# A decode step with K and V of 2048 rows streamed through a ring: the first rows of wq, V0's rows of P, the groups of the last w4 rows and the banks of the final sums

## Chip, cores and metric

One core of a Trainium2 chip. The metric is the device time of one execution in microseconds. The kernel before takes 212.08 us (median of three runs, 212.0 to 212.32); one more execution, taken with the hardware profiler, took 211.53 us.

## The reference

Four rows x (4 x 576) are normalised to xn. The result is x + A(xn) + B(xn):

```python
q = (x @ wq).reshape(B, Sq, Hq, Dh).transpose(0, 2, 1, 3)
k = jnp.repeat(k_cache[:, :, Sk - W:, :], rep, axis=1)
v = jnp.repeat(v_cache[:, :, Sk - W:, :], rep, axis=1)
p = softmax(einsum("bhqd,bhkd->bhqk", q, k) * Dh ** -0.5)
A = einsum("bhqk,bhkd->bhqd", p, v).transpose(0, 2, 1, 3).reshape(B, Sq, Hq * Dh) @ wo
B = x1 + gelu(layernorm(x1) @ w3) @ w4
```

Here W is 2048, Dh 128, with 32 query heads on 16 cache heads and 4 sequences; F is 4608. With one row per sequence the four shifted parts of the mixer (g0 to g3) are zero, so hs is zero, x1 is xn, and w1 and w2 are not needed. wq is 576 x 4096, wo 4096 x 576, w3 576 x 4608, w4 4608 x 576, all bf16. K and V give 33.5 MB each, the four matrices 20 MB: 87 MB are read for a few KB of result.

## The kernel before

All large inputs go through one SBUF tile, `ring`, by transfers that SP issues one after the other (L113, L500, L577). In order: wq in two pieces, w3, eight K tiles, two pairs of V tiles, four single V tiles, wo, 18 rows of w4, and w4's other 18 rows in groups of 7, 6, 3 and 2 (a row here is one of the 36 rows of w4 that a partition holds; the last two come in two column halves). A cache tile is 128 partitions x 32 KB and lies in one of four slots; SP's wait before a transfer is for the last reader of the place it overwrites.

*q.* x is normalised on DVE, cast, copied apart and transposed by PE (L188 to L203) into `xnT`. 36 matmuls of 512 columns (L233) add q up in one PSUM bank, in half rows of wq: wq lies in SBUF with 4.5 rows in a partition, so each half row has its own columns of `xnT`.

*K.* DVE transposes each K tile in four operations (L292), PE adds the scores up in four banks S0 to S3 (L301), one for each K tile of a half of the heads.

*P and V.* ACT takes four exponentials (L344, one per bank). `pick_rows` (L350) is eight matmuls of 512 columns that bring P's rows to the partitions on which V's rows lie; `keep_rows` (L358) copies them to `CB` on ACT; `spread_rows` (L367) makes a block matrix X from them in four DVE operations, and `v_compute` (L380) runs 64 matmuls of 256 columns for a V tile. X has two buffers. From L534 on, the order on PE, ACT and DVE is the order of the program text.

*The order behind V2.* PE zeroes a second bank ACC2 (L554); x + xn lies in the first bank, ACC, since the start (L271). The GELU of w3's product, and for the second half of the heads `heads_out`, `heads_rows` and `heads_pick`, lead to 64 matmuls with wo (L433), and from there to w4.

*The end.* `acc_matmuls` (L430) adds a row of wo or w4 to one of the two banks, even rows to ACC and odd ones to ACC2, each row in two halves of 288 columns. Four strips of the array's 128 output rows are in use so, one for each bank and half. For the last rows the sums move to four more banks `SUMS` in quarters of 144 columns: `copy_sums` (L445) copies the two banks to SBUF on ACT and DVE, `quads` (L440) adds the last 3 + 2 rows in quarters, and `merge_sums` (L449) adds the copied sums by f32 matmuls. Four casts and two output transfers (L595 to L600), one on SP and one on ACT, end the kernel.

Of the kernel before, what the change touches and what calls it, by code (L numbers as in the profile page):

```python
# [18 lines left out]
def kernel(  # L19
# [100 lines left out]
    V_order = K_order  # L120

    def k_load(n):
        bp, kq = K_order[n]
        t = ring[:, SLOT[n % 4]:SLOT[n % 4] + TILE]
        lo = Sk - W + kq * 4 * CK
        src = k_rows[MT * bp:MT * bp + MT, lo:lo + 4 * CK, :].rearrange("m (q c) d -> m q (c d)", q=4)
        return load_run(t, src).rearrange("p (c d) -> p c d", d=Dh)
# [3 lines left out]
    def v_load(n, tiles):  # L131

        bp, kq = V_order[n]
        t = ring[:, SLOT[n % 4]:SLOT[n % 4] + tiles * TILE]
        lo = Sk - W + kq // 2 * 8 * CK
        src = v_rows[MT * bp:MT * bp + MT, lo:lo + 8 * CK, :].rearrange("m (q h c) d -> m q h (c d)", q=4, h=2)
        h = kq % 2
        load_run(t, src[:, :, h:h + tiles, :].rearrange("m q h x -> m q (h x)"))
        for i in range(tiles):
            V_tiles[n + i] = t[:, i * TILE:(i + 1) * TILE].rearrange("p (c d) -> p c d", d=Dh)  # L140
# [47 lines left out]
    def transposed_prep(src_bf, name):  # L188

        dup = z_part(2 * NO * P, BF16)[0:B].rearrange("p (e o m) -> p e o m", e=2, o=NO)  # L190
        nc.gpsimd.memset(dup, 0.0)
        for e in range(2):
            nc.vector.tensor_copy(out=dup[:, e, :, e:P:2],  # L193
                                  in_=ap_of(src_bf, e * (NS // 2), [[1, NO], [NS, P // 2]]))
        return dup, const.tile([P, 2 * NO, B], BF16, name=name)

    def transposed_pe(prep):
        dup, T = prep
        tp = ps_tp.tile([P, 2 * NO, B], BF16, tag="tp")
        for o in range(NO):  # L200
            for e in range(2):
                nc.tensor.transpose(out=tp[:, 2 * (NO - 1 - o) + e, :], in_=dup[:, e, o, :], identity=ident[0:B, 0:B])  # L202
        nc.vector.tensor_copy(out=T[:], in_=tp[:])  # L203

    def slot_cols(T, s):

        return T[:, NS - 1 - s:NS + 1 - s, :].rearrange("p e b -> p (e b)")

# [20 lines left out]
    transposed_pe(xn_prep)  # L229
    for s in range(NS):  # L230
        for i in range(QI):
            f0 = s * (NQ // 2) + i * QN
            nc.tensor.matmul(out=qp[32 * i:32 * i + 2 * B, :], lhsT=slot_cols(xn_prep[1], s), rhs=wq_t[:, f0:f0 + QN],  # L233
                             start=False, stop=False, skip_group_check=True)
# [115 lines left out]
    def pick_rows(bp, g0, g1):  # L350
        for r in range(rep):
            if (bp, r) not in CPS:
                CPS[bp, r] = ps_s.tile([P, NG * CK], F32, tag="S", name=f"C{bp}{r}")
            for q in range(4):
                nc.tensor.matmul(out=CPS[bp, r][:, g0 * CK:g1 * CK], lhsT=pick[:, bp, r, 3 - q:3 - q + P],  # L355
                                 rhs=ap_of(Z, g0 * 4 * CK + q * 2 * CK, [[8 * CK, (g1 - g0) // 2], [1, 2 * CK]]), start=(q == 0), stop=(q == 3), skip_group_check=True)
# [21 lines left out]
    V_tiles, O_tiles = {}, {}  # L378

    def v_compute(n):  # L380
        bp, g = V_order[n]
        if g == 0:
# [47 lines left out]
    def acc_matmuls(lhsT, row, half):  # L430
        for q in range(2):
            o0 = 64 * half + 32 * q
            nc.tensor.matmul(out=ACCS[half][o0:o0 + B, 0:DH], lhsT=lhsT, rhs=row[:, q * DH:(q + 1) * DH],  # L433
                             start=False, stop=False, skip_group_check=True)

    SUMS = []

    DQ = D // 4

    def quads(lhsT, rows, qs=range(4), start=False):  # L440
        for q in qs:
            nc.tensor.matmul(out=SUMS[q][32 * q:32 * q + B, 0:DQ], lhsT=lhsT, rhs=rows[:, q * DQ:(q + 1) * DQ],  # L442
                             start=start, stop=False, skip_group_check=True)

    def copy_sums():  # L445
        nc.scalar.copy(out=sums[0:64], in_=ACC[0:64, 0:DH])
        nc.vector.tensor_copy(out=sums[64:P], in_=ACCS[1][64:P, 0:DH])  # L447

    def merge_sums():  # L449
        for q in range(2):  # L450
            for z in range(2):
                g = 2 * q + z
                nc.tensor.matmul(out=SUMS[g][32 * g:32 * g + B, 0:DQ], lhsT=perm[:, q, :],  # L453
                                 rhs=sums[:, z * DQ:(z + 1) * DQ], start=False, stop=False, skip_group_check=True)
# [49 lines left out]
    perm = const.tile([P, 2, B], F32)  # L504
    nc.vector.memset(perm[:].rearrange("p q m -> p (q m)"), 0.0)
    for h in range(2):
        for q in range(2):
            p0 = 64 * h + 32 * q
            nc.vector.tensor_copy(out=perm[p0:p0 + 32, q, :], in_=ident[p0:p0 + 32, p0:p0 + B])

    def mlp_out(t, e, i0, n):
# [22 lines left out]
    with tc.manual_schedule(engines=ENGINES):  # L534
        for g in range(NG):
            exponentials(g)
        pick_rows(0, 0, NG)
# [8 lines left out]
        for n in range(1, NV):  # L546
            v_compute(n)
            if n == 1:
                pick_rows(1, 0, NG)
                keep_rows(1, 0, NG)  # L550
                reciprocal_rows()
            if n == 2:
                ACCS.append(ps_s.tile([P, 512], F32, tag="S", name="ACC2"))
                nc.tensor.matmul(out=ACCS[1][:], lhsT=ident[:], rhs=zeros[:], start=True, stop=False, skip_group_check=True)  # L554
# [10 lines left out]
            if n + 4 < NV:  # L565
                v_load(n + 4, 1)
            if n == 5:
# [6 lines left out]
                last = ring[:, REST + (i0 - E1[0]) * D:REST + (NFH - E1[0]) * D].rearrange("p (i n) -> p i n", n=D)
                for side in range(2):
                    cols = slice(side * DH, (side + 1) * DH)
                    nc.sync.dma_start(out=last[:, :, cols], in_=w4_src[1, :, i0:NFH, cols])  # L577
# [13 lines left out]
        l2, l1 = [(gT[:, 2 * NFH - 2 + i, :], last[:, i, :]) for i in range(2)]
        for (g, t), q in ((l2, 0), (l1, 0), (l2, 1), (l1, 1), (l2, 2), (l2, 3), (l1, 2), (l1, 3)):
            quads(g, t, (q,))

    fins = [const.tile([B, DH], out.dtype, name=f"fin{side}") for side in range(2)]  # L595
    for q, copy in enumerate((nc.scalar.copy, nc.vector.tensor_copy, nc.vector.tensor_copy, nc.scalar.copy)):
        side, z = divmod(q, 2)
        copy(out=fins[side][:, z * DQ:(z + 1) * DQ], in_=SUMS[q][32 * q:32 * q + B, 0:DQ])  # L598
# [32 lines left out]
```

## Time and profile before

| | |
|---|---|
| median of three runs | 212.08 us |
| the profiled execution | 211.53 us |
| its span | 209.6 us |
| PE busy | 123.2 us, 59% |
| DVE busy | 130.1 us, 62% |
| ACT busy | 15.1 us |
| mean granted clock of TensorE | 0.757 |
| bytes read | 87.17 MB, 416 GB/s over the span |
| share of the 16 DMA engines that SP's queue took | 97.0% |
| first transfer issued | 0.74 us |
| K tiles landed | 37.81 to 105.9 us |
| V0 starts, V2 starts, V7 ends | 125.95, 144.56, 190.36 us |
| matmuls with wo, with w4 | from 194.06, from 200.18 us |

How to read it: an execution is measured once, from the first to the last instruction. Busy time is summed for each engine over the span. Behind an instruction in the timeline stand its tiles (out<-in), its shape, and in brackets how long its engine was idle ahead of it and what ended that. DMA shares are means of sixteen engines; in half microseconds they jump, because a packet counts where it ends.

### The profile page before, as it was taken

Reading aid. Unit: us, or ns where it says so; the run is one execution under the profiler, and the core shown is the slowest. Engines: PE = TensorE matmul, PEld = TensorE weight load, DVE = VectorE, ACT = ScalarE, POOL = GpSimd, SP = SyncE. Lnnn points to the kernel's source line nnn. Section 1 sums busy time; section 2 is a strip of 40 time slices with the busy share of each in tenths; the row PEclk is TensorE's granted clock in tenths of the full one; section 3 lists DMA queues with packets and bytes.
Section 4 is the critical chain, followed back from the end, with each engine's and each line's share of the span. In section 5 each row is a group of like instructions: output and inputs, shape, how many; then the busy total and the mean of one; then the engine's idle time right before and its main releaser. Section 6 shows DMA issues by size and latency. Waiting matters only on the chain.

```text
span 209.6 us, 2462 instructions
## 1 busy us (share of the span) xinstructions
PE 123.2 (59%) x1086; PEld 74.2 (35%) x1086; DVE 130.1 (62%) x125; ACT 15.1 (7%) x42; POOL 4.0 (2%) x10
## 2 busy tenths in 40 slices
PE   1234289143535333333333369995999997994762
PEld 0011111011111111111111118874888986883431
DVE  6952100799898989899999229976075599402002
ACT  4002100100000000000000340002001010001001
POOL 6100000000000000000000000000000000000000
PEclk9999999755555555555555559998899999999557
DMA  7998999999999999999999999999999999999991
GB/s 257 438 460 388 460 410 438 444 419 438 444 419 438 436 419 432 450 419 425 469 413 466 488 425 400 400 428 413 444 422 432 444 422 425 437 418 426 421 386 53
DMA packets 3745, 87.31 MB, mean 417 GB/s; under 512 B 396, under 2 KB 920, under 8 KB 1432
## 3 DMA queue, kind: packets, MB, share of 16 engines
q1 hardware_dynamic: 3720, 87.17, 97.0%
q8 instruction: 8, 0.13, 0.2%
q10 hardware_dynamic: 16, 0.01, 0.0%
q14 instruction: 1, 0.01, 0.0%
HBM read 87.17 MB, written 0.00 MB: 416 GB/s over the span
## 4 chain that ended last, share of the span: by engine, by line
DMA 70%; PE 19%; DVE 8%; issue 1%; SPq 1%; DVEq 0%
DMA ring<-in_A_k_cache_dram 29%; DMA ring<-in_B_w_dram 26%; PE O L386 14%; DMA ring<-in_A_v_cache_dram 14%; DVE kt L292 8%; PE G L468 4%; SPq L113 0%; SPq L500 0%; DVE mx L278 0%; PE SUM L442 0%; PE OX L416 0%; DVEq L626 0%; DVE fin L598 0%; PE SUM L453 0%; PE ACC L554 0%
## 5 line engine op out<-in xcount | busy, mean ns | idle before, releaser
L292 DVE STREAM_TRANSPOSE kt<-ring 128x2048 int32<-128x2048 int32 x32 | 71.4, 2283 | 18.7 <-DMA ring<-in_A_k_cache_dram 18.6
L386 PE MATMUL O<-ring,X 128*128 128x256 bf16 x512 | 58.4, 277 | 2.7 <-DVE X L373 1.7
L301 PE MATMUL S<-kt,Z 128*32 128x512 bf16 x256 | 30.4, 622 | 49.7 <-DVE kt L292 49.7
L386 PEld LDWEIGHTS <-X 128*128 128x128 bf16 x512 | 50.6, 99 | 10.4 <-DVE X L373 3.7
L373 DVE TENSOR_TENSOR X<-Z,own 128x1024 int32<-128x1024 int32 x32 | 36.9, 1219 | 18.9 <-issue 8.7
L301 PEld LDWEIGHTS <-Z 128*32 128x32 bf16 x256 | 10.1, 127 | 70.3 <-issue 70.3
L468 PE MATMUL G<-ring,ln2T 128*8 128x512 bf16 (+1 forms) x54 | 10.5, 862 | 2.2 <-DMA ring<-in_B_w_dram 2.2
L421 DVE TENSOR_TENSOR Z<-OX,own_d 128x256 f32<-128x256 f32 x2 | 0.8, 425 | 14.2 <-PE OX L416 14.2
L344 ACT ACTIVATE Z<-S,nb 128x512 bf16<-128x512 f32 x4 | 2.7, 694 | 80.7 <-DVE nb L531 80.7
L447 DVE COPY Z<-ACC 64x288 f32<-64x288 f32 x1 | 0.5, 461 | 12.3 <-PE ACC L433 12.3
L355 PE MATMUL C<-Z,pick 128*128 128x512 bf16 x16 | 5.5, 504 | 3.4 <-ACT Z L344 3.4
L468 PEld LDWEIGHTS <-ln2T 128*8 128x8 bf16 x54 | 2.1, 98 | 11.9 <-issue 11.0
L433 PE MATMUL ACC<-ring,gT 128*4 128x288 bf16 x62 | 3.9, 405 | 3.3 <-DMA ring<-in_B_w_dram 3.2
L202 PE MATMUL tp<-ident,Z 4*128 4x4 bf16 x20 | 1.1, 164 | 7.6 <-DVE Z L193 7.6
L433 PE MATMUL ACC<-ring,onx 128*4 128x288 bf16 x64 | 4.0, 442 | 2.2 <-DMA ring<-in_A_wo_dram 2.2
L233 PE MATMUL qp<-ring,xnT 128*8 128x512 bf16 x36 | 4.2, 621 | 1.7 <-DMA ring<-in_A_wq_dram 1.4
L244 DVE CAST q_rows<-qp 128x256 bf16<-128x256 f32 x4 | 1.5, 420 | 5.5 <-PE qp L233 4.7
L360 ACT CAST Z<-C 128x128 bf16<-128x128 f32 (+2 forms) x6 | 3.0, 543 | 18.0 <-PE C L355 17.9
L355 PEld LDWEIGHTS <-pick 128*128 128x128 bf16 x16 | 1.9, 119 | 6.6 <-issue 5.8
L202 PEld LDWEIGHTS <-Z 4*128 4x128 bf16 x20 | 0.8, 101 | 9.1 <-DVE Z L193 5.6
L433 PEld LDWEIGHTS <-gT 128*4 128x4 bf16 x62 | 2.0, 109 | 5.4 <-issue 4.2
L278 DVE TENSOR_REDUCE mx<-S 128x1 f32<-128x512 f32 x4 | 2.7, 671 | 2.0 <-PE S L301 2.0
(82 smaller groups left out, 47.2 us busy)
## 6 DMA issues: line engine op xcount, KB each, us to landing
ring<-in_A_k_cache_dram SPq DMA_DIRECT2D x8, 4096.0 KB, 35.6
ring<-in_A_v_cache_dram SPq DMA_DIRECT2D x4, 4096.0 KB, 22.3
ring<-in_B_w_dram SPq DMA_DIRECT2D x1, 5184.0 KB, 25.1
ring<-in_A_wo_dram SPq DMA_DIRECT2D x1, 4608.0 KB
ring<-in_A_wq_dram SPq DMA_DIRECT2D x1, 4096.0 KB
ring<-in_B_w_dram SPq DMA_DIRECT2D x1, 2592.0 KB, 26.8
ring<-in_B_w_dram SPq DMA_DIRECT2D x1, 1008.0 KB, 27.5
ring<-in_B_w_dram SPq DMA_DIRECT2D x1, 864.0 KB, 29.3
```

What stands on the lines that cost most here:

```text
L202: nc.tensor.transpose(out=tp[:, 2 * (NO - 1 - o) + e, :], in_=dup[:, e, o, :], identity=ident[0:B, 0:B])
L233: nc.tensor.matmul(out=qp[32 * i:32 * i + 2 * B, :], lhsT=slot_cols(xn_prep[1], s), rhs=wq_t[:, f0:f0 + QN], start=False, stop=False, skip ...
L278: nc.vector.reduce_max(out=mx[:, g:g + 1], in_=S[g][:], axis=AX.X)
L292: nc.vector.transpose(out=ap32(kt[e], c0 * 2 * G, [[2 * G, C2 // 2], [1, 2], [2, G]]), in_=ap32(kn, c0 * 4 * G + e * G, [[4 * G, C2 // 2], ...
L301: nc.tensor.matmul(out=S[kq][c:c + 32, :].rearrange("p (c q l) -> p c q l", q=4, l=2), lhsT=qz[:, bp, m, y, :], rhs=kt[e][:, :, 4 * m:4 * ...
L344: nc.scalar.activation(out=EP[:, g].rearrange("p q (c l) -> p c q l", l=2), in_=S[g][:].rearrange("p (c q l) -> p c q l", q=4, l=2), func= ...
L355: nc.tensor.matmul(out=CPS[bp, r][:, g0 * CK:g1 * CK], lhsT=pick[:, bp, r, 3 - q:3 - q + P], rhs=ap_of(Z, g0 * 4 * CK + q * 2 * CK, [[8 * ...
L360: nc.scalar.copy(out=CB[:, bp, g0:g1, :, r], in_=CPS[bp, r][:, g0 * CK:g1 * CK].rearrange("p (g c) -> p g c", c=CK))
L373: nc.vector.tensor_tensor(out=ap32(X, a * CX * MT, [[MT, CX], [1, MT]]), in0=bass.AP(s32.tensor, s32.offset, [list(s32.ap[0]), [1, CX], [0 ...
L386: nc.tensor.matmul(out=O_tiles[bp][:], lhsT=X[:, c:c + 2, :].rearrange("p c n -> p (c n)"), rhs=vn[:, c:c + 2, :].rearrange("p c d -> p (c ...
L433: nc.tensor.matmul(out=ACCS[half][o0:o0 + B, 0:DH], lhsT=lhsT, rhs=row[:, q * DH:(q + 1) * DH], start=False, stop=False, skip_group_check= ...
L468: nc.tensor.matmul(out=G_banks[k][32 * c:32 * c + 2 * B, 0:n * P].rearrange("p (i m) -> p i m", m=P), lhsT=slot_cols(ln2_prep[1], s), rhs= ...
```

## The change

- wq: its last 64 rows come first, as 128 half rows, then the other 512 rows with four whole rows in a partition. Four transposes read xn with a stride of four and two make the half rows; `xnT` has zeros between its columns.
- Cache tiles: K and V are loaded by one function with one layout. In the first half of the heads a tile takes every second 32 KB piece of a 256 KB stretch; in the second half it takes a closed one.
- V0's rows of P: with K in V's layout, the first bank alone holds V0's rows. They are picked right after the first exponential (eight matmuls of 128 columns into a bank `first`), copied after the third, and V0's first 32 matmuls run before the other rows are picked.
- The sums: ACC takes the first half of the columns, ACC2 the second, each with two sums (even rows on strips 0 or 32, odd rows on 64 or 96). x + xn's second half is copied to ACC2 behind its zeroing.
- w4's last 18 rows come in groups of 13, 3 and 2. Behind the 13 rows, the odd sums are copied to SBUF, the 3 rows go to the even sums, then the copied sums, then the 2 rows, all in the same two banks.
- Two casts and one output transfer, on ACT.

```diff
-    E1 = (7, 6, 3, 2)
-    GAP = max(0, wo_n + E0_N + E1[0] * D - 2 * TILE)
-    SLOT = [0, TILE, 2 * TILE + GAP, 3 * TILE + GAP]
-    REST = SLOT[3] + TILE
+    E1 = (13, 3, 2)
+    SLOT = [i * TILE for i in range(4)]
+    REST = 4 * TILE
...
+        src = src.rearrange("m (q h c) d -> m q h (c d)", q=4, h=2) if bp == 0 else \
+            src.rearrange("m (h q c) d -> m q h (c d)", q=4, h=2)
+        src = src[:, :, kq % 2:kq % 2 + count, :]
...
-    for a, b in ((0, NQ // 2), (NQ // 2, wq_n)):
-        load_run(wq_t[:, a:b], flat(A_wq, wq_n)[:, a:b])
+    load_run(wq_t[:, 0:WT], A_wq[KJ * P:D, :].rearrange("r (e f) -> (r e) f", e=2))
+    load_run(wq_t[:, WT:wq_n], flat(A_wq, wq_n - WT))
...
-    def acc_matmuls(lhsT, row, half):
+    def acc_matmuls(lhsT, row, par):
         for q in range(2):
-            o0 = 64 * half + 32 * q
-            nc.tensor.matmul(out=ACCS[half][o0:o0 + B, 0:DH], lhsT=lhsT, rhs=row[:, q * DH:(q + 1) * DH],
+            o0 = 64 * par + 32 * q
+            nc.tensor.matmul(out=ACCS[q][o0:o0 + B, 0:DH], lhsT=lhsT, rhs=row[:, q * DH:(q + 1) * DH],
                              start=False, stop=False, skip_group_check=True)
...
     def copy_sums():
-        nc.scalar.copy(out=sums[0:64], in_=ACC[0:64, 0:DH])
-        nc.vector.tensor_copy(out=sums[64:P], in_=ACCS[1][64:P, 0:DH])
+        for q, copy in enumerate((nc.scalar.copy, nc.vector.tensor_copy)):
+            copy(out=sums[odd_rows(q)], in_=ACCS[q][odd_rows(q), 0:DH])
     def merge_sums():
...
+            nc.tensor.matmul(out=ACCS[q][32 * q:32 * q + B, 0:DH], lhsT=perm[odd_rows(q), :], rhs=sums[odd_rows(q)],
+                             start=False, stop=False, skip_group_check=True)
...
-        for g in range(NG):
-            exponentials(g)
-        pick_rows(0, 0, NG)
-        keep_rows(0, 0, 1)
+        exponentials(0)
+        first = ps_s.tile([P, rep, CK], F32, tag="S", name="first")
+        for r in range(rep):
+            pick_rows(0, 0, 1, r, first[:, r, :])
+        exponentials(1)
+        exponentials(2)
+        for r in range(rep):
+            nc.scalar.copy(out=CB[:, 0, 0, :, r], in_=first[:, r, :])
+        exponentials(3)
+        spread_rows(0)
+        v_compute(0, 0, CK // 2)
+        pick_all(0)
         keep_rows(0, 1, NG)
-        spread_rows(0)
-        v_compute(0)
+        v_compute(0, CK // 2, CK)
...
                 nc.tensor.matmul(out=ACCS[1][:], lhsT=ident[:], rhs=zeros[:], start=True, stop=False, skip_group_check=True)
+                nc.vector.tensor_copy(out=ACCS[1][32:32 + B, 0:DH], in_=xn_f[:, DH:D])
...
-        for part in [w4_e0] + end[:2]:
-            mlp_out(*part)
+        mlp_out(*w4_e0)
+        mlp_out(*end[0])
         copy_sums()
-        t, e, i0, n = end[2]
-        for i in range(n):
-            quads(gT[:, e * NFH + i0 + i, :], t[:, i, :], start=i == 0)
+        mlp_out(*end[1], par=lambda i: 0)
         merge_sums()
...
+        mlp_out(*end[2], par=lambda i: 0)
...
+    for q, copy in enumerate((nc.scalar.copy, nc.vector.tensor_copy)):
+        copy(out=fin[:, q * DH:(q + 1) * DH], in_=ACCS[q][32 * q:32 * q + B, 0:DH])
+    nc.scalar.dma_start(out=o2, in_=fin[:])
```

More of the change, by code (lines that the diff above doesn't have):

```diff
@@ L52 @@
     NS = 9
+    KJ = 4
     NO = NS // 2 + 1
@@ L104 @@
     E0_N = NFH * D
-    E1 = (7, 6, 3, 2)
-    GAP = max(0, wo_n + E0_N + E1[0] * D - 2 * TILE)
-    SLOT = [0, TILE, 2 * TILE + GAP, 3 * TILE + GAP]
-    REST = SLOT[3] + TILE
-    RING = max(SLOT[2] + wq_n + w3_n, REST + sum(E1[1:]) * D)
+    E1 = (13, 3, 2)
+    SLOT = [i * TILE for i in range(4)]
+    REST = 4 * TILE
+    RING = max(SLOT[2] + wq_n + w3_n, REST + E1[0] * D)
+    assert wo_n + E0_N + sum(E1[1:]) * D <= 2 * TILE
     ring = ringp.tile([P, RING], BF16, tag="ring", name="ring")
@@ L119, with cache_load @@
     K_order = [(bp, kq) for bp in range(2) for kq in range(4)]
-    V_order = K_order
-    def k_load(n):
+    v_rows = A_v_cache.rearrange("b h s d -> (b h) s d")
+    def cache_load(rows, n, count, tiles):
         bp, kq = K_order[n]
[L124 to L127, printed above, removed]
-    v_rows = A_v_cache.rearrange("b h s d -> (b h) s d")
[L131 to L140, printed above, removed]
+        t = ring[:, SLOT[n % 4]:SLOT[n % 4] + count * TILE]
+        src = rows[MT * bp:MT * bp + MT, Sk - W + kq // 2 * 8 * CK:Sk - W + (kq // 2 + 1) * 8 * CK, :]
+        src = src.rearrange("m (q h c) d -> m q h (c d)", q=4, h=2) if bp == 0 else \
+            src.rearrange("m (h q c) d -> m q h (c d)", q=4, h=2)
+        src = src[:, :, kq % 2:kq % 2 + count, :]
+        load_run(t, src.rearrange("m q h x -> m q (h x)") if count > 1 else src[:, :, 0, :])
+        for i in range(count):
+            tiles[n + i] = t[:, i * TILE:(i + 1) * TILE].rearrange("p (c d) -> p c d", d=Dh)
+    K_tiles, V_tiles = {}, {}
     w4_src = B_w4.rearrange("(e m i) n -> e m i n", e=2, i=NFH)
@@ L145 @@
     assert NT == 1
+    WT = NQ // 2
     wq_t = ring[:, SLOT[2]:SLOT[2] + wq_n]
-    for a, b in ((0, NQ // 2), (NQ // 2, wq_n)):
-        load_run(wq_t[:, a:b], flat(A_wq, wq_n)[:, a:b])
+    load_run(wq_t[:, 0:WT], A_wq[KJ * P:D, :].rearrange("r (e f) -> (r e) f", e=2))
+    load_run(wq_t[:, WT:wq_n], flat(A_wq, wq_n - WT))
     w3_t = load_run(ring[:, SLOT[2] + wq_n:SLOT[2] + wq_n + w3_n], flat(B_w3, w3_n))
@@ L186, in z_part, with half_rows @@
         return Z[:, a:a + n] if dt is BF16 else Zf[:, a // 2:a // 2 + n]
-    def transposed_prep(src_bf, name):
-        dup = z_part(2 * NO * P, BF16)[0:B].rearrange("p (e o m) -> p e o m", e=2, o=NO)
+    def half_rows(src_bf, k0, step, count):
+        dup = z_part(2 * count * P, BF16)[0:B].rearrange("p (e o m) -> p e o m", e=2, o=count)
         nc.gpsimd.memset(dup, 0.0)
@@ L193, in transposed_prep, with turned @@
             nc.vector.tensor_copy(out=dup[:, e, :, e:P:2],
[L194 to L207, printed above, removed]
+                                  in_=ap_of(src_bf, k0 + e * (step // 2), [[1, count], [step, P // 2]]))
+        return dup
+    def turned(src, count, name):
+        tp = ps_tp.tile([P, count, B], BF16, tag="tp", name=name)
+        for k in range(count):
+            nc.tensor.transpose(out=tp[:, k, :], in_=src(k), identity=ident[0:B, 0:B])
+        return tp
     qz = z_part(2 * NM * NY * G, BF16).rearrange("p (a m y n) -> p a m y n", a=2, m=NM, y=NY)
     layernorm(xn_f, xn_bf, x_bf)
-    xn_prep = transposed_prep(xn_bf, "xnT")
+    x_dup = half_rows(xn_bf, KJ * P, 1, 1)
+    xnT = const.tile([P, 2 * KJ + 3, B], BF16)
+    nc.gpsimd.memset(xnT[:], 0.0)
     nc.vector.memset(Zf[:, 0:NM * NY * G], 0.0)
@@ L228 @@
     nc.tensor.matmul(out=qp[:], lhsT=ident[:], rhs=zeros[:], start=True, stop=False, skip_group_check=True)
[L229 to L234, printed above, removed]
+    tpx = turned(lambda k: xn_bf[:, k:KJ * P:KJ] if k < KJ else x_dup[:, k - KJ, 0, :], KJ + 2, "tpx")
+    nc.vector.tensor_copy(out=xnT[:, 1:2 * KJ:2, :], in_=tpx[:, 0:KJ, :])
+    nc.vector.tensor_copy(out=xnT[:, 2 * KJ + 1:2 * KJ + 3, :], in_=tpx[:, KJ:KJ + 2, :])
+    for j in range(-1, KJ):
+        for h in range(2 if j >= 0 else 1):
+            k = 2 * j + 1 - h if j >= 0 else 2 * KJ + 1
+            for i in range(QI):
+                f0 = (j * NQ + WT if j >= 0 else 0) + h * WT + i * QN
+                nc.tensor.matmul(out=qp[32 * i:32 * i + 2 * B, :], lhsT=xnT[:, k:k + 2, :].rearrange("p e b -> p (e b)"),
+                                 rhs=wq_t[:, f0:f0 + QN], start=False, stop=False, skip_group_check=True)
     q_rows = ktp.tile([P, HB, NY, NG, G], BF16, tag="kt", name="q_rows")
@@ L267 @@
     layernorm(None, ln2_bf, xn_bf)
-    ln2_prep = transposed_prep(ln2_bf, "ln2T")
+    l_dup = half_rows(ln2_bf, 0, NS, NO)
+    ln2T = const.tile([P, 2 * NO, B], BF16)
     nc.vector.tensor_tensor(out=xn_f[:], in0=xn_f[:], in1=x_bf[:], op=ALU.add)
-    for q in range(2):
-        nc.vector.tensor_copy(out=ACC[32 * q:32 * q + B, 0:DH], in_=xn_f[:, q * DH:(q + 1) * DH])
-    transposed_pe(ln2_prep)
+    nc.vector.tensor_copy(out=ACC[0:B, 0:DH], in_=xn_f[:, 0:DH])
+    tpl = turned(lambda k: l_dup[:, k % 2, NO - 1 - k // 2, :], 2 * NO, "tpl")
+    nc.vector.tensor_copy(out=ln2T[:], in_=tpl[:])
     S = []
@@ L282, in k_scores @@
         bp, kq = K_order[n]
-        kn = k_load(n)
+        cache_load(k_rows, n, 1, K_tiles)
+        kn = K_tiles.pop(n)
         if n == 0:
@@ L348, with pick_rows, pick_all @@
     CPS = {}
-    def pick_rows(bp, g0, g1):
-        for r in range(rep):
[L352 to L356, printed above, removed]
+    def pick_rows(bp, g0, g1, r, out):
+        for q in range(4):
+            nc.tensor.matmul(out=out, lhsT=pick[:, bp, r, 3 - q:3 - q + P],
+                             rhs=EP[:, g0:g1, q, :], start=(q == 0), stop=(q == 3), skip_group_check=True)
+    def pick_all(bp):
+        for r in range(rep):
+            CPS[bp, r] = ps_s.tile([P, NG * CK], F32, tag="S", name=f"C{bp}{r}")
+            pick_rows(bp, 0, NG, r, CPS[bp, r][:])
     def keep_rows(bp, g0, g1):
@@ L367, in spread_rows @@
     def spread_rows(n):
-        bp, g = V_order[n]
+        bp, g = K_order[n]
         X = ktp.tile([P, CK, PB], BF16, tag="kt", name=f"X{n}")
@@ L376, in spread_rows, with v_compute @@
         X_tiles[n] = X
[L378 to L382, printed above, removed]
+    O_tiles = {}
+    def v_compute(n, c0=0, c1=CK):
+        bp, g = K_order[n]
+        if g == 0 and c0 == 0:
             O_tiles[bp] = ps_o.tile([P, 2 * Dh], F32, tag="O", name=f"O{bp}")
         X, vn = X_tiles[n], V_tiles[n]
-        for c in range(0, CK, 2):
+        for c in range(c0, c1, 2):
             nc.tensor.matmul(out=O_tiles[bp][:], lhsT=X[:, c:c + 2, :].rearrange("p c n -> p (c n)"),
@@ L428, with odd_rows @@
     ACCS = [ACC]
-    def acc_matmuls(lhsT, row, half):
+    def acc_matmuls(lhsT, row, par):
         for q in range(2):
-            o0 = 64 * half + 32 * q
-            nc.tensor.matmul(out=ACCS[half][o0:o0 + B, 0:DH], lhsT=lhsT, rhs=row[:, q * DH:(q + 1) * DH],
+            o0 = 64 * par + 32 * q
+            nc.tensor.matmul(out=ACCS[q][o0:o0 + B, 0:DH], lhsT=lhsT, rhs=row[:, q * DH:(q + 1) * DH],
                              start=False, stop=False, skip_group_check=True)
[L436 to L443, printed above, removed]
+    def odd_rows(q):
+        return slice(64 + 32 * q, 64 + 32 * q + B)
     def copy_sums():
-        nc.scalar.copy(out=sums[0:64], in_=ACC[0:64, 0:DH])
-        nc.vector.tensor_copy(out=sums[64:P], in_=ACCS[1][64:P, 0:DH])
+        for q, copy in enumerate((nc.scalar.copy, nc.vector.tensor_copy)):
+            copy(out=sums[odd_rows(q)], in_=ACCS[q][odd_rows(q), 0:DH])
     def merge_sums():
         for q in range(2):
[L451 to L454, printed above, removed]
+            nc.tensor.matmul(out=ACCS[q][32 * q:32 * q + B, 0:DH], lhsT=perm[odd_rows(q), :], rhs=sums[odd_rows(q)],
+                             start=False, stop=False, skip_group_check=True)
     G_banks = []
@@ L468, in g_all @@
                     nc.tensor.matmul(out=G_banks[k][32 * c:32 * c + 2 * B, 0:n * P].rearrange("p (i m) -> p i m", m=P),
-                                     lhsT=slot_cols(ln2_prep[1], s), rhs=rhs, start=False, stop=False,
+                                     lhsT=ln2T[:, NS - 1 - s:NS + 1 - s, :].rearrange("p e b -> p (e b)"), rhs=rhs, start=False, stop=False,
                                      skip_group_check=True)
@@ L501, in load_w4, with mlp_out @@
         return t.rearrange("p (i n) -> p i n", n=D), e, i0, n
[L504 to L511, printed above, removed]
+    perm = const.tile([P, B], F32)
+    for q, copy in enumerate((nc.scalar.copy, nc.vector.tensor_copy)):
+        copy(out=perm[odd_rows(q), :], in_=ident[odd_rows(q), odd_rows(q)])
+    def mlp_out(t, e, i0, n, par=lambda i: i % 2):
         for i in range(n):
-            acc_matmuls(gT[:, e * NFH + i0 + i, :], t[:, i, :], i % len(ACCS))
+            acc_matmuls(gT[:, e * NFH + i0 + i, :], t[:, i, :], par(i))
     g_all()
@@ L523 @@
             k_scores(n)
-    NV = len(V_order)
-    v_load(0, 2)
-    v_load(2, 2)
+    NV = len(K_order)
+    for n in range(0, 4, 2):
+        cache_load(v_rows, n, 2, V_tiles)
     bank_max(NG - 1)
@@ L534 @@
     with tc.manual_schedule(engines=ENGINES):
-        for g in range(NG):
-            exponentials(g)
-        pick_rows(0, 0, NG)
-        keep_rows(0, 0, 1)
+        exponentials(0)
[10 more added lines that the diff above has]
+        pick_all(0)
         keep_rows(0, 1, NG)
-        spread_rows(0)
-        v_compute(0)
-        v_load(NV // 2, 1)
+        v_compute(0, CK // 2, CK)
+        cache_load(v_rows, 4, 1, V_tiles)
         spread_rows(1)
@@ L548 @@
             if n == 1:
-                pick_rows(1, 0, NG)
+                pick_all(1)
                 keep_rows(1, 0, NG)
@@ L565 @@
             if n + 4 < NV:
-                v_load(n + 4, 1)
+                cache_load(v_rows, n + 4, 1, V_tiles)
             if n == 5:
@@ L570 @@
                 end, i0 = [], 0
-                for k, m in enumerate(E1[:3]):
-                    end.append(load_w4(wo_n + E0_N if k == 0 else REST + (i0 - E1[0]) * D, 1, i0, m))
+                for k, m in enumerate(E1):
+                    end.append(load_w4(REST if k == 0 else wo_n + E0_N + (i0 - E1[0]) * D, 1, i0, m))
                     i0 += m
[L574 to L577, printed above, removed]
         heads_out(1)
         heads_pick(1, heads_rows(1))
-        SUMS += [(ps_o if g == 3 else ps_s).tile([P, 512], F32, tag="O" if g == 3 else "S", name=f"SUM{g}")
-                 for g in range(4)]
         for x in range(XR):
             acc_matmuls(onx[:, 0, x, :], wo_t[:, x * D:(x + 1) * D], x % 2)
-        for part in [w4_e0] + end[:2]:
-            mlp_out(*part)
+        mlp_out(*w4_e0)
+        mlp_out(*end[0])
         copy_sums()
-        t, e, i0, n = end[2]
-        for i in range(n):
-            quads(gT[:, e * NFH + i0 + i, :], t[:, i, :], start=i == 0)
+        mlp_out(*end[1], par=lambda i: 0)
         merge_sums()
[L591 to L598, printed above, removed]
-    for side, queue in enumerate((nc.sync, nc.scalar)):
-        queue.dma_start(out=o2[:, side * DH:(side + 1) * DH], in_=fins[side][:])
+        mlp_out(*end[2], par=lambda i: 0)
+    fin = const.tile([B, D], out.dtype, name="fin")
+    for q, copy in enumerate((nc.scalar.copy, nc.vector.tensor_copy)):
+        copy(out=fin[:, q * DH:(q + 1) * DH], in_=ACCS[q][32 * q:32 * q + B, 0:DH])
+    nc.scalar.dma_start(out=o2, in_=fin[:])
 _INS = ['A_x', 'A_k_cache', 'A_v_cache', 'A_wq', 'A_wo', 'B_x', 'B_w1', 'B_w2', 'B_w3', 'B_w4']
```

## The prediction

> **What bounds the kernel now.** I read the 40 slices first, then the waits of the DMA queue, then the timeline of the last 14 us and the clock by half microseconds, then the timeline between the last K tile and the third V tile.
>
> ```profile
> PEclk9999999755555555555555559998899999999557
> DMA  7998999999999999999999999999999999999991
> GB/s 257 438 460 388 460 410 438 444 419 438 444 419 438 436 419 432 450 419 425 469 413 466 488 425 400 400 428 413 444 422 432 444 422 425 437 418 426 421 386 53
> ```
>
> The DMA row is at 9 from the second slice to the 39th: the sixteen DMA engines stream about 430 GB/s without a hole, and 87 MB at that rate are 203 us of the 209.6. So an edit counts only if it shortens that stream, makes a hole in it, or lengthens what follows its last bytes. PE, DVE and ACT work in the middle is free as long as it keeps ahead of the stream. What follows the stream:
>
> ```profile
> 194.06 4.01 PE L433 MATMUL ACC<-ring,onx 128*4 128x288 bf16 x64 [2.17 <-DMA ring<-in_A_wo_dram]
> 200.18 3.44 PE L433 MATMUL ACC<-ring,gT 128*4 128x288 bf16 x50 [2.11 <-DMA ring<-in_B_w_dram]
> 204.74 0.54 PE L433 MATMUL ACC<-ring,gT 128*4 128x288 bf16 x12 [1.12 <-DMA ring<-in_B_w_dram]
> 205.31 0.39 ACT L446 COPY Z<-ACC 64x288 f32<-64x288 f32 x1 [14.18 <-PE ACC L433]
> 205.35 0.46 DVE L447 COPY Z<-ACC 64x288 f32<-64x288 f32 x1 [12.26 <-PE ACC L433]
> 205.83 0.36 PE L442 MATMUL SUM<-ring,gT 128*4 128x144 bf16 x12 [0.55 <-DMA ring<-in_B_w_dram]
> 206.01 0.42 PE L453 MATMUL SUM<-Z,perm 128*4 128x144 f32 x8
> 206.26 0.63 PE L442 MATMUL SUM<-ring,gT 128*4 128x144 bf16 x8
> 206.63 0.63 DVE L598 CAST fin<-SUM 4x144 bf16<-4x144 f32 x2 [0.81 <-PE SUM L442]
> 207.34 0.28 ACTq L600 DMA_DIRECT2D out_dram<-fin  x1
> ```
>
> Each group of w4 rows starts when its bytes land: 18 and 7 rows as one run of 50 matmuls at 200.18, 6 rows at 204.74, 3 rows at 205.83. The 6-row group and the copies of the sums end at 205.81, so the 3 rows never wait for them; the last cast ends at 207.26 and the output transfer goes out at 207.34. The clock in that stretch:
>
> ```profile
> 200.00:200.50 0.50, 0.32 (x8) 0.22 (x11) 0.00 (x0) 0.00 (x0) 0.00 (x0) 0.50 0.93 389
> 203.00:203.50 0.50, 0.50 (x14) 0.26 (x3) 0.00 (x0) 0.00 (x0) 0.00 (x0) 0.63 1.01 392
> 203.50:204.00 0.50, 0.12 (x2) 0.00 (x0) 0.00 (x0) 0.00 (x0) 0.00 (x0) 1.00 0.97 353
> 206.50:207.00 0.50, 0.34 (x6) 0.09 (x3) 0.34 (x2) 0.32 (x2) 0.00 (x0) 0.79 0.00 0
> ```
>
> The column after POOL is the granted clock: 0.50 until about 203.4, 1.00 until about 206.8. The run of 50 matmuls, 3.4 us without a pause, came just before it rose; the 64 matmuls from 194.06 to 198.07 had not raised it.
>
> ```profile
> 120.72 3.57 PE L355 MATMUL C<-Z,pick 128*128 128x512 bf16 x8 [3.38 <-ACT Z L344]
> 144.56 8.81 PE L386 MATMUL O<-ring,X 128*128 128x256 bf16 x64 [1.04 <-DMA ring<-in_A_v_cache_dram]
> 153.21 0.38 PE L554 MATMUL ACC<-zeros,ident 128*128 128x512 bf16 x1
> ```
>
> V2 starts when its transfer lands at 144.56, whatever V0 and V1 did before.
>
> **The change part by part.** The sum is made against the profiled execution: span 209.6, time 211.53 (1.9 outside the span). The three timed runs have a median of 212.08, 0.55 above it.
>
> *wq and x.* Two transfers of the same bytes in the same order of sizes (512 KB, then 4 MB). Six transposes replace ten and shorter copies replace two of 0.68 us; all of it lies before 14.50, when PE waits for the bulk of wq. q is ready near 24, and the first K tile lands at 37.81. Nothing; without that 13 us of cover it would gain below 2.
>
> *Layout of the cache tiles.* K's first four tiles take the strides V has (32 KB pieces, 64 KB apart), the last four V tiles take K's closed rows. Five K tiles land from 37.81 to 86.48, 9.73 us each (431 GB/s); the four strided V tiles with wo take 21.50 MB from 144.56 to 194.06 (434 GB/s). A swap: I take 0, and the bounds are 8 tiles by the difference of 0.07 us, -0.6 to +0.6.
>
> *V0 picked ahead.* X0 can start at about 121.2 (three exponentials by 120.55, two copies of 0.30) where it started at 124.67. But V0's own transfer lands at about 125.2: K7 lands at 105.9, and 8.39 MB more take 19.3. So V0 gains at most 0.7. Against it, the eight matmuls of 512 columns that kept PE busy from 120.72 to 124.29 move into the middle of V0. The clock went up right behind them; eight of 128 columns last a quarter (0.9 us). V0 then starts at half clock. 256 columns take 0.110 at full clock (14.15 for 128) and twice that at half, so V0 loses 1.5 to 3 us until the clock rises. From 125.2, V0 with a pick of 1.8 inside ends near 135.6, V1 near 142.6, and V2 starts 3.7 later as before (picks, copies, reciprocals), at 146.3 in place of 144.56.
>
> *The copy of x into the second bank.* On DVE it stands ahead of X3's four operations, and it waits for the zeroing matmul behind V2. X3 was made at 140.14 and cost nothing. Now it starts at 153.6 + 0.45, its first quarter is ready 1.16 later, near 155.3, and V3 starts 1.9 late; X4 and later follow. If the pause costs a stretch of half clock too, another 1.7. V7, done at 190.36, is done at 192.3 to 194.3.
>
> *What hides both.* wo's matmuls are ready 2.8 behind V7 (190.36 to 193.14): 195.1 to 197.1, where they started at 194.06. They last 4.0 at half clock; the 18 rows then take 2.4 and end by 203.5 at the latest, before 204.74. The transfers issued behind V3 and V5 have a backlog of over 7 us (V7's was issued at 160.6 and its turn is at 173.7). So nothing; beyond 1.2 us more, it would move the end one for one.
>
> *Rows 13, 3, 2.* The 7- and 6-row groups become one, which lands when the 6 did: 204.74. Where 12 matmuls were left at that moment, 26 are. Their price: 12 of 288 columns took 0.54 and 12 of 144 columns 0.36, so 0.030 each and 0.18 for the last result to come out, at full clock; at half, the 36 of the 18 rows ran from 200.18 to 202.61, where the next weights were loaded, 0.067 each. 26 are 0.96 or 1.92. Then the copies, 0.46 with 0.05 around them: 4 rows instead of 64, but as many elements in each, so I leave it.
>
> *One bank for each half.* The 3 rows no longer go to banks of their own. As the changed program is built, their first matmul waits for ACT's copy and their second for DVE's: copies and rows, side by side before, come one after the other, and the merge and the last 2 rows are queued behind on PE. All use one strip of four output rows for each half, so two matmuls run side by side, no longer four: a row costs 4 x 0.030 = 0.12 at full clock, 0.24 at half. Merges: eight f32 passes took 0.42, less 0.18, 0.24 for 144 columns; 288 take 0.48 (half clock 0.96). Were two no slower than four, the rows would cost half and the merges 0.24 (0.48): the lower bound, 0.54 less at full clock and 1.08 at half.
>
> *Output.* One cast of 288 on each of ACT and DVE, priced as the copy, 0.46; before, two of 0.31. The transfer that went out last was ACT's, and one still goes out there after both casts: 0, within 0.1. The 2 rows come in pieces of 2304 bytes instead of 576 and may land 0.2 sooner; PE is later, so this is hidden.
>
> The sum, from 204.74:
> full clock: 0.96 + 0.51 + 0.36 + 0.48 + 0.24 + 0.18 + 0.51 = 3.24, end of the cast 207.98 against 207.26: +0.7, 212.2;
> 13 rows at full clock, the rest at half: 0.96 + 0.51 + 0.72 + 0.96 + 0.48 + 0.18 + 0.51 = 4.32: +1.8, 213.3;
> half clock throughout: 1.92 + 0.51 + 0.72 + 0.96 + 0.48 + 0.18 + 0.51 = 5.28: +2.8, 214.3.
>
> Which clock? Before, the last rise needed 3.4 us without pause. After, the 18 rows are followed by nothing until 204.74, so the clock is either still low, or was raised by wo's matmuls running into the 18 rows and falls again during the tail, as it fell at 206.8. I take 213.6, between the second and the third.
>
> The Trainium skill ("TensorE: Matmul & The Clock Gate", The HAM clock gate) says that activity is judged in free-running windows of about 3.4 us which do not start with the kernel. The rows agree in size (203.4 to 206.8). By it the tail's clock would differ from run to run, before and after alike; the sums by it stay between 212.2 and 214.3.
>
> **The rivals.**
> *Full clock to the end*: 212.2. For it: the clock is 1.00 over this whole tail before. Against: a pause of 1 to 2 us ahead of the 13 rows, with more work behind it.
> *The stream gets shorter* (the other side): the 8 K tiles and the last 4 V tiles, all of them next to a changed layout, move at 441 GB/s, which the slice from 160 to 170 us reached, and not 431: 0.22 less each, 2.6 in all, 213.6 - 2.6 = 211.0. It decides from 0.16 a tile. Against: both layouts are in the trace, and differ by 0.07.
> *The serial tail is not there*: the wait on the copies is over before the rows land, and the last transfer still sets the end: 0.2 sooner, cast +0.15, 211.5. Against: 204.74 + 0.96 + 0.51 is past the 205.83 at which the rows land.
> *PE falls behind*: V0 and V3 lose 2 us more than summed, the 13 rows start at 205.7: 214.7.
>
> **How the numbers follow.** Forecast 0.61, full clock 0.18, shorter stream 0.07, no serial tail 0.07, PE behind 0.07. The forecast's own range is 212.5 (two strips no slower than four, 1.08 less) to 214.5. For 8 in 10: from 212.0, which takes in the full clock, to 214.8, with PE behind. 0.2% is 0.42 us, about what a measurement of this kernel can tell from no change: faster is below 211.66 (shorter stream, and about half of no serial tail: 0.10), the same up to 212.50 (most of full clock: 0.17), slower 0.73.
>
> **What would show it.** Right: the 13-row matmuls start near 204.7 with 1.0 to 1.9 us to go, then copies, 3 rows, merges, 2 rows in series without a wait for a DMA, the last cast near 209, DMA at 9 until 203. X3 stands behind the DVE copy, and V3 starts 2 us or more behind V2's end. Wrong: the 2 rows wait for their transfer; PE at 1.00 in the whole tail; K tiles landing closer than 9.6; the 13 rows starting late because PE still works on the 18.

## The result and the profile after

The changed kernel takes 213.57 us (median of four runs, 213.41 to 213.82) beside 212.04 for the kernel before on the same chip: a ratio of 1.0079, 95% interval 1.0051 to 1.0107. It is slower by 1.5 us.

The slices of its page first, the same rows as before:

```profile
PEclk9999559555555555555555557999999999999955
DMA  7999899999999999999999999979999999998960
GB/s 298 414 430 501 349 491 396 396 482 408 396 464 427 394 476 408 402 482 408 495 461 408 420 408 457 482 325 470 414 405 470 414 430 451 440 441 372 430 258 1
```

The stream is as full as before, but for the 27th slice at 7, and ends in the 39th of 40 slices: a whole slice (5.3 us) without transfers is left behind it. What stands there, from the timeline of the end:

```profile
195.35 2.13 PE L434 MATMUL ACC<-ring,onx 128*4 128x288 bf16 x64 [1.24 <-DVE onx L426]
199.97 1.27 PE L434 MATMUL ACC<-ring,gT 128*4 128x288 bf16 x36 [2.49 <-DMA ring<-in_B_w_dram]
204.42 1.84 PE L434 MATMUL ACC<-ring,gT 128*4 128x288 bf16 x26 [3.17 <-DMA ring<-in_B_w_dram]
206.29 0.39 ACT L442 COPY Z<-ACC 4x288 f32<-4x288 f32 x1 [12.96 <-PE ACC L434]
206.33 0.46 DVE L442 COPY Z<-ACC 4x288 f32<-4x288 f32 x1 [11.04 <-PE ACC L434]
206.74 0.99 PE L434 MATMUL ACC<-ring,gT 128*4 128x288 bf16 x6 [0.47 <-ACT Z L442]
207.65 1.12 PE L446 MATMUL ACC<-Z,perm 4*4 4x288 f32 x4
208.71 0.64 PE L434 MATMUL ACC<-ring,gT 128*4 128x288 bf16 x4
209.42 0.45 DVE L585 CAST fin<-ACC 4x288 bf16<-4x288 f32 x1 [2.63 <-PE ACC L434]
209.95 0.27 ACTq L586 DMA_DIRECT2D out_dram<-fin  x1
```

From 204.42 to 209.95 every step waits for the one ahead of it: the 6 matmuls of the 3 rows name ACT's copy (`ACT Z`) as what released them, and neither they nor the last 4 wait for a transfer. Before, the output went out 2.60 after the 6-row group had landed (204.74 to 207.34); now it goes out 5.53 after the 13 rows landed. The clock (the column after POOL, as before), in stretches of the same execution:

```profile
201.00:201.50 0.50, 0.24 (x8) 0.03 (x1) 0.00 (x0) 0.00 (x0) 0.00 (x0) 1.00 0.98 419
202.00:203.00 1.00, 0.00 (x0) 0.00 (x0) 0.00 (x0) 0.00 (x0) 0.00 (x0) 0.50 0.91 384
204.50:206.00 1.50, 1.50 (x26) 0.83 (x25) 0.00 (x0) 0.00 (x0) 0.00 (x0) 0.50 0.40 157
```

At 1.00 the 18 rows took only 1.27 us; then PE had nothing to do for 3.2 us, the clock fell, and the 13 rows found it at 0.50.

### The profile page after: what moved, and what is told of

It reads as the page before. It is cut to its first block, busy times and chain, and to the rows that moved or that the text cites. A ratio compares the mean times of both kernels' runs of the same rounds, so it can differ in the third digit from the quotient of the medians.

```text
span 212.0 us, 2437 instructions
## 1 busy us (share of the span) xinstructions
PE 121.8 (57%) x1076; PEld 74.0 (35%) x1076; DVE 128.5 (61%) x121; ACT 15.1 (7%) x42; POOL 3.2 (2%) x11
## 4 chain that ended last, share of the span: by engine, by line
DMA 62%; PE 25%; DVE 9%; issue 2%; SPq 1%; ACT 1%; DVEq 0%
DMA ring<-in_A_k_cache_dram 35%; PE O L387 20%; DMA ring<-in_A_v_cache_dram 14%; DMA ring<-in_B_w_dram 13%; DVE kt L291 7%; PE ACC L434 2%; PE C L351 2%; SPq L114 1%; DVE X L374 1%; PE ACC L446 0%; ACT Z L361 0%; DVE mx L276 0%; PE RD L400 0%; DVE fin L585 0%; PE OX L417 0%
## 5 line engine op out<-in xcount | busy, mean ns | idle before, releaser
L387 PE MATMUL O<-ring,X 128*128 128x256 bf16 x512 | 59.4, 279 | 6.5 <-DMA ring<-in_A_v_cache_dram 4.8
L434 PE MATMUL ACC<-ring,gT 128*4 128x288 bf16 x72 | 4.7, 360 | 6.1 <-DMA ring<-in_B_w_dram 5.7
L552 DVE COPY ACC<-xn_f 4x288 f32<-4x288 f32 x1 | 0.5, 453 | 11.1 <-PE ACC L551 11.1
L442 DVE COPY Z<-ACC 4x288 f32<-4x288 f32 x1 | 0.5, 462 | 11.0 <-PE ACC L434 11.0
L361 ACT CAST Z<-C 128x384 bf16<-128x384 f32 (+1 forms) x4 | 2.6, 659 | 21.5 <-PE C L351 21.3
L351 PEld LDWEIGHTS <-pick 128*128 128x128 bf16 x24 | 2.4, 111 | 4.3 <-issue 2.8
L351 PE MATMUL C<-Z,pick 128*128 128x512 bf16 x16 | 3.8, 379 | 0.0
L409 ACT ACTIVATE Z<-O,rd_rows 64x128 f32<-64x128 f32 x4 | 1.5, 363 | 29.7 <-PE O L387 29.6
L434 PE MATMUL ACC<-ring,onx 128*4 128x288 bf16 x64 | 2.1, 286 | 1.2 <-DVE onx L426 1.2
```

The source lines that it names most:

```text
L351: nc.tensor.matmul(out=out, lhsT=pick[:, bp, r, 3 - q:3 - q + P], rhs=EP[:, g0:g1, q, :], start=(q == 0), stop=(q == 3), skip_group_check= ...
L361: nc.scalar.copy(out=CB[:, bp, g0:g1, :, r], in_=CPS[bp, r][:, g0 * CK:g1 * CK].rearrange("p (g c) -> p g c", c=CK))
L387: nc.tensor.matmul(out=O_tiles[bp][:], lhsT=X[:, c:c + 2, :].rearrange("p c n -> p (c n)"), rhs=vn[:, c:c + 2, :].rearrange("p c d -> p (c ...
L434: nc.tensor.matmul(out=ACCS[q][o0:o0 + B, 0:DH], lhsT=lhsT, rhs=row[:, q * DH:(q + 1) * DH], start=False, stop=False, skip_group_check=True)
```

## The experiments

Each was timed beside the kernel before, in three series. That kernel's median was 212.05 beside `a_oldtail`, `b_newtail`, `a_fill` and `a_oddbanks`, 212.11 beside `a_split76`, `a_mid`, `b_newwq` and `a_oldtail_fill`, and 212.03 beside the other three. Of each edit the main lines are shown; "..." stands for lines left out.

**The end alone, taken out and put in.** `a_oldtail` is the changed kernel with the end of the kernel before; the copy of x ahead of X3, which belongs to the changed end, goes with it:

```diff
-    E1 = (13, 3, 2)
+    E1 = (7, 6, 3, 2)
...
-        mlp_out(*w4_e0)
-        mlp_out(*end[0])
+        for part in [w4_e0] + end[:2]:
+            mlp_out(*part)
         copy_sums()
-        mlp_out(*end[1], par=lambda i: 0)
+        t, e, i0, n = end[2]
+        for i in range(n):
+            quads(gT[:, e * NFH + i0 + i, :], t[:, i, :], start=i == 0)
         merge_sums()
-        mlp_out(*end[2], par=lambda i: 0)
...
```

> The changed kernel with the end of the kernel before: rows 7, 6, 3 and 2 with the halves of the last two, even and odd sums in a bank each, quarters in four banks, two output transfers; layout, wq, V0's pick stay changed. Theory (the series on PE from 204.4 at half clock makes the whole loss): 211.6 to 212.3, as before, the 3 rows again starting when they land. Rival (layout of the tiles, V0's pick or the copy ahead of X3 cost it): 213.3 to 213.7.

Measured: 211.39 us (211.10 to 211.66), ratio 0.9975 [0.9961, 0.9989]. The loss is gone, and the run is 0.66 faster than the kernel before, which is less than the 211.6 expected at the least.

`b_newtail` is the reverse, the kernel before with the changed end.

> The kernel before with the changed end alone: rows 13, 3, 2, a bank for each half, one output transfer, and the copy of x ahead of X3 that belongs to it. Theory: the whole loss is here, 213.3 to 213.8, 26 matmuls left when the 13 rows land near 204.7 and the clock low. Rival: 212.0 to 212.4.

Measured: 214.03 us (213.92 to 214.10), ratio 1.0098 [1.0084, 1.0112]. The end alone costs 2.0 us, half a microsecond more than the whole change. Its last 26 + 6 + 4 + 4 matmuls, copies and casts take 204.40 to 209.93, 5.53 as in the changed kernel. So the rest of the change gains about 0.5 (214.03 - 213.57) to 0.65, which the prediction had not seen.

**The clock.** `a_fill` puts matmuls that add nothing to the result, into a bank of their own, where PE was idle:

```diff
...
+        fill(8)
         mlp_out(*w4_e0)
+        fill(10)
         mlp_out(*end[0])
```

> The changed kernel with matmuls that add nothing to the result between the groups: 8 of 512 columns behind wo's matmuls and 10 behind the 18 rows, in a bank of their own, so that PE is hardly idle from 195 on. Theory: the clock is 1.00 through the end and the series takes 3.2 to 3.4 us instead of 5.5: 211.9 to 212.4. Rival 1 (the series costs what it costs, whatever the clock): 213.5. Rival 2 (the extra matmuls stand in the way of the 13 rows): above 214.

Measured: 211.61 us (211.39 to 211.95), ratio 0.9988 [0.9978, 0.9997], a little below what was expected, as `a_oldtail` was. The end in its timeline, and the clock in the stretch in which the changed kernel has 0.50:

```profile
204.42 1.02 PE L434 MATMUL ACC<-ring,gT 128*4 128x288 bf16 x26
205.91 0.64 PE L434 MATMUL ACC<-ring,gT 128*4 128x288 bf16 x6 [0.47 <-ACT Z L442]
206.48 0.65 PE L446 MATMUL ACC<-Z,perm 4*4 4x288 f32 x4
207.06 0.41 PE L434 MATMUL ACC<-ring,gT 128*4 128x288 bf16 x4
208.06 0.28 ACTq L594 DMA_DIRECT2D out_dram<-fin  x1
```

```profile
204.50:206.00 1.50, 1.03 (x27) 0.65 (x26) 0.46 (x1) 0.39 (x1) 0.00 (x0) 1.00 0.36 141
```

The 13 rows start at the same 204.42, and the same instructions take 3.64 us instead of 5.53. Nothing was taken away and work was added: the clock alone makes 1.9 us.

**The wait on the copies.** `a_oddbanks` gives the odd sums two banks of their own, so the 3 rows need not wait until the copies have read them.

```diff
-            nc.tensor.matmul(out=ACCS[q][o0:o0 + B, 0:DH], lhsT=lhsT, rhs=row[:, q * DH:(q + 1) * DH],
+            nc.tensor.matmul(out=(ODDS if par else ACCS)[q][o0:o0 + B, 0:DH], lhsT=lhsT, rhs=row[:, q * DH:(q + 1) * DH],
...
```

> The changed kernel with the odd sums in two banks of their own, so that the 3 rows do not wait for the copies. Theory: copies (0.45) and 3 rows (0.9 at half clock) lie side by side again, 0.45 to 0.6 less: 212.9 to 213.2. Rival (the wait on the copies is no part of it, the loss is the 13 rows and the clock alone): 213.4 to 213.7.

Measured: 212.75 us (212.68 to 213.00), ratio 1.0040 [1.0027, 1.0053]: 0.8 less, somewhat more than expected. The copies start as soon as the last odd row is in (205.67, 1.65 after the landing and no longer 1.87), the 3 rows run beside them, and the output goes out 4.78 after the landing (204.02 to 208.80).

**The size of the group.** `a_split76` keeps the changed banks and splits 13 into 7 and 6.

```diff
-    E1 = (13, 3, 2)
+    E1 = (7, 6, 3, 2)
...
```

> The changed kernel with groups of 7, 6, 3 and 2 rows in place of 13, 3 and 2; banks, copies and output as changed. Theory: 14 of the 26 matmuls run before the last of these rows lands, so 12 are left at 204.4; at half clock 0.9 to 1.0 us less: 212.4 to 212.8. Rival (the group's size is hidden, the series behind it alone counts): 213.4 to 213.7.

Measured: median 212.55 us over twelve runs, ratio 1.0004 [0.9986, 1.0023], but in groups: three runs from 211.09 to 211.26, one at 211.71, eight from 212.22 to 212.74. The larger group is where it was expected. The profiled run, 211.24, is one of the lower:

```profile
201.00:202.00 1.00, 0.56 (x16) 0.18 (x8) 0.00 (x0) 0.00 (x0) 0.00 (x0) 0.50 1.04 436
203.50:205.50 2.00, 0.94 (x18) 0.46 (x17) 0.47 (x1) 0.39 (x1) 0.00 (x0) 1.00 0.50 198
```

In it the clock rose just ahead of the last rows, as in the profiled run of the kernel before. No run of the upper group was profiled; that the clock stayed at half there is argued from the 1.4 us between the groups, not shown.

**The middle.** `a_mid` restores the four exponentials and all picks ahead of V0, and moves the copy of x behind X3.

```diff
...
-                nc.vector.tensor_copy(out=ACCS[1][32:32 + B, 0:DH], in_=xn_f[:, DH:D])
             if n == 3:
                 heads_out(0)
+                nc.vector.tensor_copy(out=ACCS[1][32:32 + B, 0:DH], in_=xn_f[:, DH:D])
```

> The changed kernel with the middle put back: all four exponentials and picks ahead of V0, and the copy of x into the second bank ahead of X4 in place of X3. Theory: V2 and V3 start on time again and wo's matmuls start with wo's landing, but the end stays, since it hangs on the landing of the 13 rows: 213.3 to 213.8. Rival (PE's lateness in the middle is part of the loss): 213.0 or less.

Measured: 213.68 us (213.51 to 214.03), ratio 1.0082 [1.0067, 1.0098]: the same. PE is back on time (V2 at 144.10, wo's matmuls at 193.59, released by wo's landing), and the 13 rows still start at 204.22 with the clock at 0.50. Neither the early pick nor the wait on DVE costs or gains anything.

**The head.** `b_newwq` is the kernel before with the changed order of wq.

```diff
-    for a, b in ((0, NQ // 2), (NQ // 2, wq_n)):
-        load_run(wq_t[:, a:b], flat(A_wq, wq_n)[:, a:b])
+    load_run(wq_t[:, 0:WT], A_wq[KJ * P:D, :].rearrange("r (e f) -> (r e) f", e=2))
+    load_run(wq_t[:, WT:wq_n], flat(A_wq, wq_n - WT))
...
```

> The kernel before with the changed head alone: wq's last 64 rows first, four whole rows in a partition, six transposes. With the old end the changed kernel took 211.39, 0.66 less than before, and w3 landed 0.5 sooner. Theory (the head shortens the stream): w3 lands near 26.2, 211.4 to 211.8. Rival (the layout of the cache tiles does it): 211.9 to 212.2, w3 at 26.7.

Measured: 211.82 us (210.90 to 212.09), ratio 0.9989 [0.9977, 1.0001]: 0.3 less, at the edge of what can be told, and in its profile w3 landed at 26.46, between what was expected (26.2) and the rival's 26.7. The profile of the kernel before has 1.00 in the end and that of `b_newwq` 0.50, and both kernels' ends seem to run at either clock. So it was measured again with the clock held by the extra matmuls, `b_newwq_fill` beside `b_oldtail_fill` (the kernel before and these matmuls alone).

> The kernel before with the matmuls that add nothing to the result, 8, 4 and 4 as in a_oldtail_fill, and nothing else. Theory: its own runs lie in two groups, near 211.3 and near 212.1, because the clock is full at its end in some and half in others; with the clock held they fall together at 211.3 to 211.5. Rival (the groups come from the stream): the two groups stay, median near 212.

> The same with the changed head (wq's last 64 rows first). With the clock held the head can be read: if it makes the 0.3 that b_newwq showed, 0.2 to 0.4 below b_oldtail_fill; if the layout of the tiles and V0's pick made the rest of what a_oldtail gained, it stays 0.2 or more above a_oldtail_fill's 210.89.

Measured: 211.52 us (211.16 to 211.87), ratio 0.9980 [0.9969, 0.9990], and 210.97 us (210.85 to 211.17), ratio 0.9955 [0.9941, 0.9969]. With the clock held, the runs of the kernel before near 212.1 are gone, as expected, though the rest spreads over 0.7 us. The head makes 0.55, more than the 0.2 to 0.4 expected, and `a_oldtail_fill` (210.89, below), which has the layout and the early pick too, is only 0.08 faster. The two profiles at the start of the stream and at the landing of the 3 rows, kernel with the old head first:

```profile
2.00:4.00 2.00, 1.03 (x2) 0.13 (x2) 1.61 (x7) 1.69 (x6) 0.57 (x3) 1.00 1.05 354
205.99 0.36 PE L442 MATMUL SUM<-ring,gT 128*4 128x144 bf16 x12 [0.57 <-DMA ring<-in_B_w_dram]
```

```profile
2.00:4.00 2.00, 1.01 (x2) 0.10 (x1) 1.53 (x7) 1.65 (x6) 0.33 (x1) 1.00 1.27 506
205.24 0.36 PE L446 MATMUL SUM<-ring,gT 128*4 128x144 bf16 x12 [0.54 <-DMA ring<-in_B_w_dram]
```

The last figure of each first line is GB/s. In these 2 us the first 512 KB of wq move, in 128 pieces of 4 KB, and the start of its bulk, in pieces of 32 KB: at 354 GB/s where the pieces lie 36 KB apart and at 506 where they lie side by side. The bulk of wq then releases PE at 14.66 and 13.91, w3 at 26.94 and 26.19, and the lead of 0.75 is still there when the 3 rows land, at 205.99 and 205.24.

That the head makes the gain is shown. That the place of the pieces does is argued from the GB/s: the edit changes both transfers of wq and the making of xnT at once. Nor is the lead the same in every profile. In `a_mid`, with the new head, wq and w3 release PE only at 14.51 and 26.77. The first K tile still lands at 37.06 there; over all profiles it lands from 37.06 to 37.33 with the new head (ten) and from 37.45 to 37.94 with the old one (three).

The layout of the cache tiles and the early pick add nothing: with the old end and the clock held, the kernel that has them takes 210.89, and from the first to the last K tile its profile takes 68.19 us, that of `b_newwq_fill` 68.11.

**Versions that beat both.** `a_oldtail_fill` is the changed kernel with the old end and 8, 4 and 4 extra matmuls; `a_mended` keeps the changed end, but splits the 13 rows, gives the odd sums banks of their own and adds the same matmuls.

> The changed kernel with the old end, and matmuls that add nothing to the result behind wo's (8 of 512 columns), the 18 rows (4) and the 7 rows (4). Theory: the old end at full clock hangs on the last transfer alone, 0.2 to 0.4 less than with the old end at half clock (211.39): 211.0 to 211.2. Rival (the old end hangs on the transfers at either clock): 211.3 to 211.5. If the extra matmuls get in the way: above 211.6.

> The changed kernel with its end mended: groups 7, 6, 3, 2, odd sums in banks of their own, matmuls that add nothing as above; still two strips, f32 merges of 288 columns, one output transfer. Theory: at full clock and without the wait on the copies the series is short enough to hang on the landings, 210.7 to 211.2, level with a_oldtail_fill. Rival (two strips and the long merge cost by themselves): 211.3 to 211.7.

Measured: 210.89 us (210.70 to 211.12), ratio 0.9950 [0.9935, 0.9964], and 211.13 us (211.02 to 211.32), ratio 0.9962 [0.9949, 0.9975]. Both are faster than both kernels. Against `a_oldtail` (211.39, half clock in its profile) the held clock gains the old end 0.5; its timeline:

```profile
205.37 0.36 PE L444 MATMUL SUM<-ring,gT 128*4 128x144 bf16 x12 [0.57 <-DMA ring<-in_B_w_dram]
205.55 0.42 PE L455 MATMUL SUM<-Z,perm 128*4 128x144 f32 x8
205.80 0.61 PE L444 MATMUL SUM<-ring,gT 128*4 128x144 bf16 x8
206.87 0.27 ACTq L617 DMA_DIRECT2D out_dram<-fin  x1
```

and that of the mended end:

```profile
205.23 0.53 PE L435 MATMUL ACC<-ring,gT 128*4 128x288 bf16 x6 [0.50 <-DMA ring<-in_B_w_dram]
205.69 0.65 PE L447 MATMUL ACC<-Z,perm 4*4 4x288 f32 x4
206.27 0.41 PE L435 MATMUL ACC<-ring,gT 128*4 128x288 bf16 x4
207.28 0.28 ACTq L600 DMA_DIRECT2D out_dram<-fin  x1
```

In both the 3 rows wait for their landing again. From there, two strips with a merge of 288 columns need 2.05 us until the output goes out, four strips with quarters 1.50. The extra half microsecond in the profiles shows as 0.24 between the medians.

## Why the prediction was right, and where it was not

- *The series behind the 13 rows*: right, the cause and the sign. The forecast of 213.6 was a mixture of clocks, and the profiled run had the worst of them, half clock throughout: 5.45 to the end of the cast, where the third sum had 5.28. The 26 matmuls (1.84 against 1.92), the 2 rows and the casts came as priced. The 3 rows and the merges were sized too small: 0.91 and 1.06 at half clock instead of 0.72 and 0.96, and in `a_fill` 0.57 and 0.58 instead of 0.36 and 0.48. For the 3 rows a part may be the wait for DVE's copy, which ends 0.05 after they start; where they wait for no copy (`a_mended`) they take 0.46. What makes the other 0.1 is open. It is not that a group goes to the same strips as the one ahead: in the kernel before, the 3 rows and the merges did so on four strips and took 0.18 and 0.25, what the columns give.
- *Which clock*: right that there is an idle stretch ahead of the 13 rows, wrong on the way there. PE ran late in the middle as summed (V3 at 155.63 against 155.3, wo's matmuls at 195.35 against 195.1 to 197.1), but the half-clock stretch that was allowed for V3 did not come. The clock stayed at 1.00 from about 130 to 201.8, so the 18 rows were done in 1.27 us, and PE idled 3.2 us ahead of the 13 rows. That this speed decided the clock is not shown: in `a_mid` the 18 rows ran at half clock for 2.33 us, PE idled 2.19, and the 13 rows found 0.50 as well.
- *The wait on the copies*: right; taking it away gave 0.8.
- *wq and x, "Nothing"*: this step was wrong. It counted bytes and sizes, which are the same, and not where the pieces lie in memory. It also set the head against the 13 us until the first K tile lands, while by its own first lines what counts is the stream, and there the lead is kept to the end. The head was worth 0.55, so the end costs 2.0 and the change 1.5.
- *The base*: the profiled run of the kernel before, 211.53, has full clock in its end, and its median, 0.5 above, does not stand for that. With the clock held it takes 211.52. Measured from 211.53, the end cost 2.5 (`b_newtail`, 214.03) where 2.1 was forecast, and the head gave back about 0.5. That 213.6 came so near 213.57 is luck in so far as these two errors cancel.
- *Layout, V0's pick, the copy ahead of X3, one output transfer*: nothing, as predicted; `a_mid` shows it for the middle. The output transfer was not tried by itself.

Of the rivals, the shorter stream was there, at the head instead of in the tiles, and at 0.55 instead of 2.6. Full clock to the end is what `a_fill` makes; the four profiles with the 13 rows and without extra matmuls (the changed kernel, `b_newtail`, `a_oddbanks`, `a_mid`) all have 0.50 from the 13 rows to the output. The Trainium skill ("TensorE: Matmul & The Clock Gate", The HAM clock gate) has windows of 3413 ns that do not start with the kernel. In the changed kernel's trace the clock rises near 130.1 and falls near 201.8, 21 times 3.41 apart, which agrees with it. One program, `a_split76`, ends in groups 1.4 us apart; that agrees too, if the clock makes the groups.

## What to carry to other kernels

Behind a stream that bounds the kernel, every row of work that waits for the last landings is paid in full, at the clock that the idle time ahead of it has left: keep the last groups small enough that each is done before the next lands, and do not let a copy and the next group share a bank. Work that adds nothing, put into idle stretches only, can hold TensorE's clock for the end; here it was worth 0.5 us to the kernel before and 2.0 to the changed one. When two loads move the same bytes in pieces of the same size, compare where the pieces lie, above all in the first loads of a stream that bounds the kernel.
